# Turning k and q in halves in the first layer's PSUM banks, and using idle score banks at the end

## The chip, the cores and the metric

The kernel runs on one core of a Trainium2 chip. The metric is device time in microseconds, the median of three runs: 531.08 us for the kernel before (531.07 to 531.32). Its profiled execution has a span of 530.9 us, with TensorE's clock granted in full all the way.

## What is computed

Two stages. First attention over 8 batches of 8 heads, 576 positions of 64 numbers each, in which every score that lies more than `tau` below its row's greatest is dropped; then a two-layer network on the 4608 tokens, 512 to 2048 to 512, with `h - tanh(h)` between.

```python
def _attn_ref(q, k, v, tau):
    scale = 1.0 / np.sqrt(q.shape[-1])
    scores = scale * np.matmul(q, k.transpose(0, 1, 3, 2))
    thresh = np.max(scores, axis=-1, keepdims=True) - tau
    scores = np.where(scores >= thresh, scores, -1000000000.0)
    scores = scores - np.max(scores, axis=-1, keepdims=True)
    attn = np.exp(scores)
    attn = attn / (np.sum(attn, axis=-1, keepdims=True) + 1e-09)
    return np.matmul(attn, v).astype(np.float32)

def _moe_ref(x, w_in, w_out):
    h = x @ w_in
    g = h - np.tanh(h)
    return (g @ w_out).astype(np.float32)
```

## The kernel before

The heads are taken in 32 pairs, each of 9 score tiles of 128 queries (288 tiles in all). The main loop has one **slot** for each tile. In slot s TensorE makes the scores of tile s + 8, a step of the two-layer network (below), the value products of an earlier tile, and, in some slots, the turns of k or q of a coming pair. VectorE scales the scores and takes their maxima (`sc`), ScalarE makes from them the cut scores `z` and the weights `pT` and the `tanh` of the network's hidden layer, and GpSimd splits q and k into two fp16 parts and copies k's turned matrix with its halves swapped (`kS`). From pair 6 on the weights are turned by DMA (`zT`), and from pair 8 on three q of four too.

The network is done in 8 blocks of 512 tokens and a ninth with the 64 rows that are left of each batch. An **h step** (`hidden`) is four matmuls of the first layer into a bank of `ps_h`; its tanh (`bend`) and the subtraction that gives `g` (`shrink`) are issued in the next slot, and only `shrink` lets the bank go. A **y step** (`project`) is four matmuls of the second layer into the one bank of `ps_y`; four y steps make one output tile. A block's steps lie beside the scores of later pairs; the last two blocks come after all the scores.

[...]`ps_big` has two tiles of two banks, for scores and here for turns; `ps_o` one bank for value products; `ps_h` two for the first layer, and for turning x (`psX`); `ps_y` one for the second layer. A tile with the same tag waits for the one that had its place.

```python
    ps_big = pool("ps_big", 2, space=PSUM)
    ps_o = pool("ps_o", 1, space=PSUM)
    ps_h = pool("ps_h", 2, space=PSUM)
    ps_y = pool("ps_y", 1, space=PSUM)
    # ... (cut)
    def turn(p, t):
        hl = hls.pop((p, t))
        if t == "q" and q_by_dma(p):
            m = mats[p, t] = qk_pool.tile([P, W], FP16, name=f"{t}T", tag=t)
            nc.sync.dma_start_transpose(
                out=m.rearrange("p (c r) -> p c r", c=TPP),
                in_=hl.rearrange("p c a d -> p (c a d)"),
            )
            return
        ps = ps_big.tile([P, W], FP16, name=f"ps_{t}", tag="big")
        for c in range(TPP):
            turn_chunk(
                ps[:, c * P : (c + 1) * P], c, hl[:, c, :, :].rearrange("p a d -> p (a d)")
            )
        m = qk_pool.tile([P, W], FP16, name=f"{t}T", tag=t)
        nc.vector.tensor_copy(out=m, in_=ps)
        mats[p, t] = m
        if t == "k":
            sw = qk_pool.tile([P, W], FP16, name="kS", tag="ks")
            for lo, hi in ((0, D), (D, 0)):
                o, i = sw[lo : lo + D, :], m[hi : hi + D, :]
                nc.gpsimd.tensor_copy(out=o, in_=i)
            mats[p, "ks"] = sw
    # ... (cut)
    # scores(i), cut
        ps = ps_big.tile([P, 1024], F32, name="psS", tag="big")
    # ... (cut)
        sc = sc_pool.tile([P, S], F32, name="sc")
        nc.vector.tensor_scalar(
            out=sc, in0=ps[:, lo : lo + S], scalar1=SC, scalar2=None,
            op0=ALU.mult, op1=ALU.max, accum_out=mx[:, c : c + 1],
        )
    # ... (cut)
    # attend(i), cut
        if t == 1:
            ops[p, hh] = ps_o.tile([P, 6, D + 1], F32, name="psO", tag="o")
            if p % 2 and hh == 0:
                attend_shared(p, 1, pts.pop(i - 2))
        po = ops[p, hh]
    # ... (cut)
    def hidden(m, n, ps):
        if n == 0:
            gs[m] = g_pool.tile([P, DF_C, MB], BF16, name="g")
        for c in range(DM_C):
            nc.tensor.matmul(
                out=ps, lhsT=w_in_sb[:, c, n * P : (n + 1) * P],
                rhs=xs[m][:, c, :] if m < B else xR[:, c, :, :],
                start=(c == 0), stop=(c == DM_C - 1),
            )
        halves.append((m, n, ps))

    halves, ths = [], []

    def bend():
        while halves:
            m, n, ps = halves.pop(0)
            th = t_pool.tile([P, MB], F32, name="th")
            nc.scalar.activation(out=th, in_=ps, func=ACT.Tanh)
            ths.append((m, n, ps, th))

    def shrink():
        while ths:
            m, n, ps, th = ths.pop(0)
            nc.vector.scalar_tensor_tensor(
                out=gs[m][:, n, :], in0=th, scalar=-1.0, in1=ps,
                op0=ALU.mult, op1=ALU.add,
            )
    # ... (cut)
    # layers(m, tail), cut
        def h_step(n):
            if tail and n % 2:
                ps = ps_big.tile([P, MB], F32, name="psHt", tag="big")
            else:
                ps = ps_h.tile([P, MB], F32, name="psH", tag="h")
            hidden(m, n, ps)

        def y_step(m, ms, part):
            if part == 0:

                odd = tail and (m, ms) > (B - 2, 1) and ms % 2 == 0
                pl, tag = (ps_o, "o") if odd else (ps_y, "y")
                ys[m, ms] = pl.tile([P, d_model], F32, name="psY", tag=tag), odd
            ps, odd = ys[m, ms]
            project(m, ms, part, ps, odd)
    # ... (cut)
    # the loop over slots, cut
    turns = set()
    for p in range(HPAIR + 1, NPAIR):
        d = 6 if p % 2 else 3
        turns.add(TPP * p - AHEAD - (d if p >= 5 else 5))

    # ... (cut)
            assert not todo
            todo = layers(stage, False)
            room = range(s, min(s + HPAIR * TPP, NTILE))
            if room[-1] + 1 < NTILE:
                room = [a for a in room if a not in turns]
            share = len(todo) / len(room)
            done, stage = 0.0, stage + 1
    # ... (cut)
        n = s + AHEAD
        if 0 < n < NTILE and place(n)[1] is None and kind(n) == "B":
            scores(n - 1)
        if 0 <= n < NTILE and (place(n)[1] is not None or kind(n) == "B"):
            scores(n)
    # ... (cut)
        for i in kinks.pop(s, []):
            kink(i)
        bend()
        for i in wts.pop(s, []):
            weights(i)
        if 0 <= s < NTILE + FIRST:
            if todo and (s >= NTILE or s in room):
                done += share
                if s < NTILE and s == room[-1]:
                    done = 1e9
                while todo and done >= 1:
                    todo.pop(0)()
                    done -= 1
        if s == 0:
        shrink()
    # ... (cut)
            pp, jj = divmod(i, TPP)
            if i < NTILE:
                attend(i)
                odd = pp % 2
                if jj == 3 + odd:
                    norm(pp, 0)
                elif odd and jj in (0, 8):
                    norm(pp - (jj == 0), 1)
            if pp and jj == 1 + pp % 2:
                emit_x(pp - 1)
        for step in plan.pop(s, []):
            step()
        if s + AHEAD in cast_when:
            w_cast()
        if s + AHEAD in load_when:
            w_load(next(pieces))
```

Of the kernel before, what the change touches and what calls it, by code (L numbers as in the profile page):

```python
# [9 lines left out]
F32 = mybir.dt.float32  # L10
BF16 = mybir.dt.bfloat16
FP16 = mybir.dt.float16
# [6 lines left out]
def kernel(  # L19
# [216 lines left out]
    def turn_chunk(out, c, lhsT):  # L236
# [4 lines left out]
            out=out, lhsT=lhsT, rhs=rhs, is_transpose=True, start=True, stop=True  # L241
        )

    def q_by_dma(p):

        return p >= 2 * HPAIR and p % 4 != 0
# [7 lines that stand above are left out]
                in_=hl.rearrange("p c a d -> p (c a d)"),  # L254
            )
            return
        ps = ps_big.tile([P, W], FP16, name=f"ps_{t}", tag="big")
        for c in range(TPP):
            turn_chunk(
                ps[:, c * P : (c + 1) * P], c, hl[:, c, :, :].rearrange("p a d -> p (a d)")  # L260
            )
        m = qk_pool.tile([P, W], FP16, name=f"{t}T", tag=t)
        nc.vector.tensor_copy(out=m, in_=ps)
        mats[p, t] = m
        if t == "k":
            sw = qk_pool.tile([P, W], FP16, name="kS", tag="ks")
# [4 lines that stand above are left out]
# [138 lines left out]
    def attend(i):  # L409

        if kind(i) == "A":
            return
        p, hh, t = place(i)
        vb, pt = vbs[p % NV], pts[i]
        if hh is None:

            attend_shared(p - 1, 0, pt)
            return
        if t == 1:
            ops[p, hh] = ps_o.tile([P, 6, D + 1], F32, name="psO", tag="o")  # L420
            if p % 2 and hh == 0:
                attend_shared(p, 1, pts.pop(i - 2))
        po = ops[p, hh]

        nc.tensor.matmul(  # L425
            out=po[:, t - 1 : t + 1, :], lhsT=pt[:, 4 * P : 5 * P],
            rhs=vb[:, hh, 4:6, :], start=True, stop=False, skip_group_check=True,
        )
        for n in range(8):
            ab, c = divmod(n, 4)  # L430
            blk = 5 * ab + c
            nc.tensor.matmul(  # L432
                out=po[:, t - 1 + ab, :], lhsT=pt[:, blk * P : (blk + 1) * P],
                rhs=vb[:, hh, c, :], start=False, stop=(n == 7), skip_group_check=True,
            )
        pts.pop(i)
# [113 lines left out]
                    )  # L550


    EARLY = lambda m: 3 if m else 3
    LAST = 1

    FIRST = 3
    quarters = lambda m: [(m, ms, part) for ms in range(4) for part in range(4)]

    def layers(m, tail):


        def h_step(n):
# [8 lines that stand above are left out]

                odd = tail and (m, ms) > (B - 2, 1) and ms % 2 == 0
                pl, tag = (ps_o, "o") if odd else (ps_y, "y")
                ys[m, ms] = pl.tile([P, d_model], F32, name="psY", tag=tag), odd
            ps, odd = ys[m, ms]
            project(m, ms, part, ps, odd)

        def y_half(h):

            n = d_model // 2  # L580
            pl, tag = ((ps_y, "y"), (ps_o, "o"))[h]
            ps = pl.tile([P, n], F32, name="psY", tag=tag)
            for part in range(4):
                project(m, 3, part, ps, h == 0, slice(h * n, h * n + n))

        now = quarters(m - 1)[EARLY(m - 1) :] if m > 0 else []
        if m < NMB - 1:
            now += quarters(m)[: EARLY(m)]
        else:
            now += quarters(m)[:12]  # L590
        n = 16 + len(now)


        ahead = n - max(0, EARLY(m) - 3) - LAST if m < NMB - 1 else n - 9 - LAST
        steps, at, i = [], [], 0

        def ready(y):
            last = 4 * y[2] + 3
            return y[0] < m or len(at) > (last if m else 15) and at[last] + 2 < i

        while now or len(at) < 16:
            if len(at) < 16 and (
                not now or not ready(now[0]) or len(at) * ahead <= i * 16
            ) and not (m == B - 1 and i < FIRST):
                steps.append(lambda a=len(at): h_step(a))
                at.append(i)
            elif ready(now[0]):
                steps.append(lambda y=now.pop(0): y_step(*y))
            else:
                steps.append(lambda: None)  # L610
            i += 1
        if m == NMB - 1:
            steps += [lambda h=h: y_half(h) for h in range(2)]
        return steps

    ys = {}


    def w_pieces():
# [39 lines left out]
    for p in range(1, NPAIR):  # L659
        first = TPP * p - AHEAD  # L660
        for d, f in PREP[3 if p == 1 else 0 :]:
            d -= p == 1 and d in (3, 5)
            if d in (7, 8) and q_by_dma(p):
                d = d + 2
            if p in (2, 4):
                d = {8: 9, 7: 8, 5: 6}.get(d, d)
            elif d == 5 and p >= 5:
                d = 6 if p % 2 else 3
            plan.setdefault(first - d, []).append(lambda p=p, f=f: f(p))
        d = 7 if q_by_dma(p) else 3 - (p == 1 or p >= 5)  # L670
        d = 4 if p in (2, 4) else d
        plan.setdefault(first - d, []).append(lambda p=p: turn(p, "q"))
# [21 lines left out]

    turns = set()
    for p in range(HPAIR + 1, NPAIR):
        d = 6 if p % 2 else 3
        turns.add(TPP * p - AHEAD - (d if p >= 5 else 5))  # L700

    kinks, wts, atts = {}, {}, {}
    for i in range(NTILE + 3):
# [5 lines left out]
    for s in range(-AHEAD, NTILE + LAG + 3):  # L709
        p, j = divmod(max(s, 0), TPP)  # L710
        if 0 <= s < NTILE and j == 2 + LAG and p % HPAIR == 0 and p >= HPAIR:
            assert not todo
            todo = layers(stage, False)
            room = range(s, min(s + HPAIR * TPP, NTILE))
            if room[-1] + 1 < NTILE:
                room = [a for a in room if a not in turns]
            share = len(todo) / len(room)
            done, stage = 0.0, stage + 1
        if s == NTILE:
            todo = layers(stage, True)  # L720
            share, done, stage = 1, 0.0, stage + 1
        if 0 <= s + AHEAD - 1 < NTILE:
            shift(s + AHEAD - 1)

# [5 lines that stand above are left out]
        if s == 1 - AHEAD:  # L730
            for t in ("k", "q", "ks"):
                turn_first(t, 1)
        for i in kinks.pop(s, []):
            kink(i)
        bend()
        for i in wts.pop(s, []):
            weights(i)
        if 0 <= s < NTILE + FIRST:
            if todo and (s >= NTILE or s in room):
                done += share  # L740
                if s < NTILE and s == room[-1]:
                    done = 1e9
                while todo and done >= 1:
                    todo.pop(0)()
                    done -= 1
        if s == 0:
            nc.vector.tensor_tensor(
                out=fold, in0=ident_bf[:, 0:64], in1=ident_bf[:, 64:P], op=ALU.add
            )
        shrink()  # L750
        for store in stores[:-1]:
            store()
        del stores[:-1]
        for i in atts.pop(s, []):
# [14 lines that stand above are left out]
        if s + AHEAD in load_when:  # L769
            w_load(next(pieces))  # L770

    for step in todo:
        step()
        bend()
        shrink()
# [49 lines left out]
```

## Time and profile before

| | PE | DVE | ACT | POOL |
|---|---|---|---|---|
| busy, us of 530.9 | 507.7 | 422.1 | 433.4 | 289.3 |
| share | 96% | 80% | 82% | 54% |

PE is TensorE, PEld its weight loads (which lie beside its matmuls), DVE VectorE, ACT ScalarE, POOL GpSimd. Lines such as L331 are lines of the kernel; a name pair `psS<-kT,qT` is what an instruction writes and what it reads, `x2` how many instructions one row of a timeline stands for. A bracket at a row's end gives the engine's idle time before it and whose work ended it. Matmuls are pipelined and their ends are modelled, so two neighbouring matmuls overlap in the profile; their starts are firm.

Some durations that the text uses:

| row | instruction | count | mean ns |
|---|---|---|---|
| L341 | DVE scales a tile of scores, `sc<-psS` | 288 | 753 |
| L517 | DVE `g<-th,psH` | 128 | 684 |
| L263 | DVE `kT<-ps_k`, 1152 columns | 31 | 751 |
| L537 | DVE `yo<-psY` | 30 | 691 |
| L458 | DVE `osb<-psO,rc` (norm; with its reciprocal, 177) | 64 | 424 |
| L511 | ACT `th<-psH` | 128 | 583 |
| L368 | ACT `z<-sc` | 288 | 769 |
| L404 | ACT `pT<-zT` | 117 | 1154 |

### The profile page before, as it was taken

The page shows a single profiled execution, that of the slowest core. Times are in us where ns is not written, and L with a number is a line of the kernel's source. Part 1 is how long each engine was busy: PE and PEld are TensorE (multiplying, and loading weights), DVE is VectorE, ACT ScalarE, POOL GpSimd, SP SyncE. Part 2 cuts the span into 40 slices and gives each one's busy share as a digit, 9 for nine tenths or more (in the row PEclk, how much of TensorE's full clock was granted, in tenths as well). Part 3 has the DMA queues.
Part 4 walks back from the last instruction along what each step waited for, and adds up shares of the span by engine and source line. Part 5 has one row for each costly group of instructions (what it writes and reads, how often), then busy time and mean ns, then how long its engine had stood idle before and what let it go on. Part 6 is the DMA issues. An engine that isn't in the chain of part 4 may idle for free.

```text
span 530.9 us, 12707 instructions
## 1 busy us (share of the span) xinstructions
PE 507.7 (96%) x4606; PEld 286.4 (54%) x4606; DVE 422.1 (80%) x1179; ACT 433.4 (82%) x617; POOL 289.3 (54%) x390
## 2 busy tenths in 40 slices
PE   8999899989999989999999999999999999999996
PEld 4666566554555545555555555555555555444444
DVE  5999889997898878998889888888899887554440
ACT  5999999998898989988998989899998989544330
POOL 7999999684738366574738383846657430000000
PEclk9999999999999999999999999999999999999999
DMA  7843668989799999899998999999988976400113
GB/s 215 242 141 112 216 214 168 184 145 201 180 199 162 183 181 202 167 193 205 180 198 180 199 175 216 157 198 185 204 169 196 202 133 110 105 36 25 39 41 80
DMA packets 208607, 86.79 MB, mean 163 GB/s; under 512 B 176160, under 2 KB 200992, under 8 KB 208544
## 3 DMA queue, kind: packets, MB, share of 16 engines
q1 hardware_dynamic: 207952, 85.56, 77.4%
q8 instruction: 36, 0.59, 0.5%
q10 hardware_dynamic: 592, 0.43, 0.3%
q14 instruction: 27, 0.22, 0.1%
HBM read 36.70 MB, written 9.44 MB: 87 GB/s over the span
## 4 chain that ended last, share of the span: by engine, by line
PE 48%; issue 13%; ACT 12%; DVE 12%; POOL 7%; DMA 7%; SPq 1%; ACTq 0%; POOLq 0%; DVEq 0%
PE psY L524 15%; PE psH L498 12%; PE psS L331 9%; ACT z L368 5%; DVE sc L341 4%; ACT pT L396 3%; DMA zT<-z 3%; PE psHt L498 3%; DVE g L517 2%; PE psO L432 2%; ACT th L511 2%; POOL kS L269 2%; ACT pT L404 2%; DMA vraw<-in_v_dram 2%; PE psS L322 2%
## 5 line engine op out<-in xcount | busy, mean ns | idle before, releaser
L341 DVE TENSOR_SCALAR_CACHE_REDUCE sc<-psS 128x576 f32<-128x576 f32 x288 | 212.9, 753 | 34.2 <-PE psS L331 21.3
L368 ACT ACTIVATE z<-sc,nb 128x576 bf16<-128x576 f32 x288 | 216.0, 769 | 27.6 <-DVE nb L353 27.1
L524 PE MATMUL psY<-w_out_sb,g 128*128 128x512 bf16 (+1 forms) x592 | 146.0, 374 | 0.8 <-DVE yo L537 0.8
L404 ACT ACTIVATE pT<-zT 128x1152 f16<-128x1152 bf16 x117 | 135.0, 1154 | 10.6 <-DMA zT<-z 10.4
L269 POOL COPY kS<-kT 64x1152 f16<-64x1152 f16 x62 | 70.8, 1142 | 125.4 <-DVE nb L353 123.7
L498 PE MATMUL psH<-xT,w_in_sb 128*128 128x512 bf16 x480 | 123.3, 379 | 0.7 <-DVE g L517 0.3
L331 PEld LDWEIGHTS <-qT 128*128 128x128 f16 x1024 | 75.1, 97 | 67.3 <-issue 11.8
L331 PE MATMUL psS<-kT,qT 128*128 128x512 f16 (+1 forms) x512 | 104.3, 285 | 7.2 <-DVE sc L341 4.0
L517 DVE SCALAR_TENSOR_TENSOR g<-th,psH 128x512 bf16<-128x512 f32 x128 | 87.6, 684 | 25.5 <-ACT th L511 23.6
L331 PE MATMUL psS<-kS,qT 128*128 128x512 f16 x496 | 101.3, 286 | 1.7 <-POOL kS L269 1.6
L511 ACT ACTIVATE th<-psH 128x512 f32<-128x512 f32 x128 | 74.6, 583 | 21.9 <-PE psH L498 21.8
L524 PEld LDWEIGHTS <-g 128*128 128x128 bf16 x592 | 51.0, 98 | 57.2 <-issue 3.5
L498 PEld LDWEIGHTS <-w_in_sb 128*128 128x128 bf16 x576 | 48.8, 98 | 53.2 <-issue 1.0
L432 PE MATMUL psO<-vb,pT 128*128 128x65 bf16 x1024 | 53.3, 194 | 0.0
L432 PEld LDWEIGHTS <-pT 128*128 128x128 f16 x1024 | 44.2, 98 | 9.4
L193 POOL TENSOR_TENSOR khl<-kraw,khl 128x576 f16<-128x576 f32 x31 | 39.7, 1281 | 2.6
L193 POOL TENSOR_TENSOR qhl<-qraw,qhl 128x576 f16<-128x576 f32 x31 | 39.7, 1280 | 2.6
L396 ACT ACTIVATE pT<-psZ 128x512 f16<-128x512 bf16 (+1 forms) x54 | 35.1, 654 | 2.6 <-PE psZ L387 2.1
L537 DVE COPY yo<-psY 128x512 f32<-128x512 f32 (+1 forms) x31 | 21.1, 682 | 13.6 <-PE psY L524 12.4
L458 DVE TENSOR_TENSOR osb<-psO,rc 128x256 bf16<-128x256 f32 x64 | 27.2, 424 | 2.2
L425 PE MATMUL psO<-vb,pT 128*128 128x130 bf16 x128 | 28.1, 220 | 0.6 <-DVE nb L353 0.6
L387 PE MATMUL psZ<-ident_bf,z 128*128 128x128 bf16 x243 | 22.5, 220 | 2.1 <-ACT pT L396 1.3
(79 smaller groups left out, 509.5 us busy)
## 6 DMA issues: line engine op xcount, KB each, us to landing
vraw<-in_v_dram SPq DMA_DIRECT2D x32, 256.0 KB, 3.6
out_dram<-yo SPq DMA_DIRECT2D x32, 256.0 KB, 3.1
kraw<-in_k_dram SPq DMA_DIRECT2D x31, 256.0 KB, 3.1
qraw<-in_q_dram SPq DMA_DIRECT2D x31, 256.0 KB, 3.4
wt<-in_moe_w_in_dram SPq DMA_DIRECT2D x8, 512.0 KB, 4.6
wt<-in_moe_w_out_dram SPq DMA_DIRECT2D x8, 512.0 KB, 4.2
zT<-z SPq DMA_TRANSPOSE x117, 3.7
qraw<-in_q_dram SPq DMA_DIRECT2D x32, 32.0 KB, 3.1
```

Source lines behind the costliest of these rows:

```text
L193: nc.gpsimd.tensor_tensor(out=hl[:, :, 1, :], in0=x, in1=hl[:, :, 0, :], op=ALU.subtract)
L269: nc.gpsimd.tensor_copy(out=o, in_=i)
L331: nc.tensor.matmul(out=ps[:, dst], lhsT=lhs, rhs=kk[:, src], start=(n == 0), stop=(n == 1),)
L341: nc.vector.tensor_scalar(out=sc, in0=ps[:, lo : lo + S], scalar1=SC, scalar2=None, op0=ALU.mult, op1=ALU.max, accum_out=mx[:, c : c + 1],)
L368: nc.scalar.activation(out=z, in_=sc, func=ACT.Prelu, bias=nb, scale=1.0, alpha=STEEP)
L396: nc.scalar.activation(out=pt[:, off * P : (off + n) * P], in_=ps[:, 0 : n * P], func=ACT.Exp)
L404: nc.scalar.activation(out=pt[:, 0 : n * P], in_=zts.pop(i)[:, 0:n, :], func=ACT.Exp)
L432: nc.tensor.matmul(out=po[:, t - 1 + ab, :], lhsT=pt[:, blk * P : (blk + 1) * P], rhs=vb[:, hh, c, :], start=False, stop=(n == 7), skip_gr ...
L498: nc.tensor.matmul(out=ps, lhsT=w_in_sb[:, c, n * P : (n + 1) * P], rhs=xs[m][:, c, :] if m < B else xR[:, c, :, :], start=(c == 0), stop= ...
L511: nc.scalar.activation(out=th, in_=ps, func=ACT.Tanh)
L517: nc.vector.scalar_tensor_tensor(out=gs[m][:, n, :], in0=th, scalar=-1.0, in1=ps, op0=ALU.mult, op1=ALU.add,)
L524: nc.tensor.matmul(out=ps, lhsT=gs[m][:, n, ms * P : (ms + 1) * P], rhs=w_out_sb[:, n, cols], start=(n == 0), stop=(n == DF_C - 1),)
```

## The change

From pair 6 on, k, and q where TensorE turns it, are no longer turned as nine chunks in one tile of the score banks with one copy out. They go as five chunks and four, in two tiles of the first layer's pool `ps_h`, each with its own copy. That leaves both score tiles to the scores. k's turn is moved: for even pairs it comes one slot earlier, for odd ones one slot later, so that it falls on a slot without value products.

The network's steps are no longer spread by a running share. A list of slots (without those in which k is turned) is given to `layers`, which puts an h step or a y step on each: h steps are spread so that they end five slots before the list does, a y step is preferred in the slot just before a turn, and what is left goes into the last slot. In the last score stage the slots of turns are now left out too, so 29 slots are there for 32 steps.

Two tiles move to the score banks at the end, where scores are over: the value products of the last pair, and the first output tile of block 6.

```diff
--- before.py
+++ after.py
@@ -241,6 +241,14 @@
             out=out, lhsT=lhsT, rhs=rhs, is_transpose=True, start=True, stop=True
         )
 
+
+    BYHALF = HPAIR + 2
+
+    def k_lead(p):
+        if p < BYHALF:
+            return 6 if p in (2, 4) or p == HPAIR + 1 else 5 - (p == 1)
+        return 5 if p % 2 else 4
+
     def q_by_dma(p):
 
         return p >= 2 * HPAIR and p % 4 != 0
@@ -254,13 +262,20 @@
                 in_=hl.rearrange("p c a d -> p (c a d)"),
             )
             return
-        ps = ps_big.tile([P, W], FP16, name=f"ps_{t}", tag="big")
-        for c in range(TPP):
-            turn_chunk(
-                ps[:, c * P : (c + 1) * P], c, hl[:, c, :, :].rearrange("p a d -> p (a d)")
-            )
         m = qk_pool.tile([P, W], FP16, name=f"{t}T", tag=t)
-        nc.vector.tensor_copy(out=m, in_=ps)
+        if p < BYHALF:
+            spans, pl, tag = ((0, TPP),), ps_big, "big"
+        else:
+            spans, pl, tag = ((0, 5), (5, TPP)), ps_h, "h"
+        for c0, c1 in spans:
+            n = (c1 - c0) * P
+            ps = pl.tile([P, n], FP16, name=f"ps_{t}", tag=tag)
+            for c in range(c0, c1):
+                turn_chunk(
+                    ps[:, (c - c0) * P : (c - c0 + 1) * P], c,
+                    hl[:, c, :, :].rearrange("p a d -> p (a d)"),
+                )
+            nc.vector.tensor_copy(out=m[:, c0 * P : c1 * P], in_=ps)
         mats[p, t] = m
         if t == "k":
             sw = qk_pool.tile([P, W], FP16, name="kS", tag="ks")
@@ -417,7 +432,9 @@
             attend_shared(p - 1, 0, pt)
             return
         if t == 1:
-            ops[p, hh] = ps_o.tile([P, 6, D + 1], F32, name="psO", tag="o")
+
+            pl, tag = (ps_big, "big") if p == NPAIR - 1 else (ps_o, "o")
+            ops[p, hh] = pl.tile([P, 6, D + 1], F32, name="psO", tag=tag)
             if p % 2 and hh == 0:
                 attend_shared(p, 1, pts.pop(i - 2))
         po = ops[p, hh]
@@ -550,13 +567,14 @@
                     )
 
 
-    EARLY = lambda m: 3 if m else 3
+    EARLY = lambda m: 3
     LAST = 1
 
     FIRST = 3
     quarters = lambda m: [(m, ms, part) for ms in range(4) for part in range(4)]
 
-    def layers(m, tail):
+
+    def layers(m, tail, slots=None):
 
 
         def h_step(n):
@@ -571,6 +589,8 @@
 
                 odd = tail and (m, ms) > (B - 2, 1) and ms % 2 == 0
                 pl, tag = (ps_o, "o") if odd else (ps_y, "y")
+                if (m, ms) == (B - 2, 0):
+                    pl, tag = ps_big, "big"
                 ys[m, ms] = pl.tile([P, d_model], F32, name="psY", tag=tag), odd
             ps, odd = ys[m, ms]
             project(m, ms, part, ps, odd)
@@ -597,6 +617,21 @@
         def ready(y):
             last = 4 * y[2] + 3
             return y[0] < m or len(at) > (last if m else 15) and at[last] + 2 < i
+
+        if slots is not None:
+            for nth, i in enumerate(slots):
+                spare = len(slots) - nth - (16 - len(at)) - len(now)
+                can = now and ready(now[0]) and (m or i >= CAST_BY[now[0][2]])
+                due = len(at) * (len(slots) - OWN(m)) <= nth * 16
+                lull = i + 1 not in slots and spare >= 0
+                if len(at) < 16 and not (can and (lull or not due)) and (due or spare <= 0):
+                    steps.append((i, lambda a=len(at): h_step(a)))
+                    at.append(i)
+                elif can:
+                    steps.append((i, lambda y=now.pop(0): y_step(*y)))
+            assert len(at) == 16 and all(ready(y) for y in now)
+            steps += [(i, lambda y=y: y_step(*y)) for y in now]
+            return steps
 
         while now or len(at) < 16:
             if len(at) < 16 and (
@@ -616,6 +651,10 @@
     ys = {}
 
 
+    CAST_BY = (56, 56, 58, 64)
+    OWN = lambda m: EARLY(m) + 2
+
+
     def w_pieces():
         for w, sb, n in ((moe_w_in, w_in_sb, DM_C), (moe_w_out, w_out_sb, DF_C)):
             flat = sb.rearrange("p c n -> p (c n)")
@@ -659,13 +698,13 @@
     for p in range(1, NPAIR):
         first = TPP * p - AHEAD
         for d, f in PREP[3 if p == 1 else 0 :]:
-            d -= p == 1 and d in (3, 5)
+            d -= p == 1 and d == 3
             if d in (7, 8) and q_by_dma(p):
                 d = d + 2
-            if p in (2, 4):
-                d = {8: 9, 7: 8, 5: 6}.get(d, d)
-            elif d == 5 and p >= 5:
-                d = 6 if p % 2 else 3
+            if d == 5:
+                d = k_lead(p)
+            elif p in (2, 4):
+                d = {8: 9, 7: 8}.get(d, d)
             plan.setdefault(first - d, []).append(lambda p=p, f=f: f(p))
         d = 7 if q_by_dma(p) else 3 - (p == 1 or p >= 5)
         d = 4 if p in (2, 4) else d
@@ -694,10 +733,7 @@
 
 
 
-    turns = set()
-    for p in range(HPAIR + 1, NPAIR):
-        d = 6 if p % 2 else 3
-        turns.add(TPP * p - AHEAD - (d if p >= 5 else 5))
+    turns = {TPP * p - AHEAD - k_lead(p) for p in range(HPAIR + 1, NPAIR)}
 
     kinks, wts, atts = {}, {}, {}
     for i in range(NTILE + 3):
@@ -710,15 +746,12 @@
         p, j = divmod(max(s, 0), TPP)
         if 0 <= s < NTILE and j == 2 + LAG and p % HPAIR == 0 and p >= HPAIR:
             assert not todo
-            todo = layers(stage, False)
             room = range(s, min(s + HPAIR * TPP, NTILE))
-            if room[-1] + 1 < NTILE:
-                room = [a for a in room if a not in turns]
-            share = len(todo) / len(room)
-            done, stage = 0.0, stage + 1
+            todo = layers(stage, False, [a for a in room if a not in turns])
+            stage += 1
         if s == NTILE:
-            todo = layers(stage, True)
-            share, done, stage = 1, 0.0, stage + 1
+            todo = [(s + n, step) for n, step in enumerate(layers(stage, True))]
+            stage += 1
         if 0 <= s + AHEAD - 1 < NTILE:
             shift(s + AHEAD - 1)
 
@@ -735,14 +768,8 @@
         bend()
         for i in wts.pop(s, []):
             weights(i)
-        if 0 <= s < NTILE + FIRST:
-            if todo and (s >= NTILE or s in room):
-                done += share
-                if s < NTILE and s == room[-1]:
-                    done = 1e9
-                while todo and done >= 1:
-                    todo.pop(0)()
-                    done -= 1
+        while todo and todo[0][0] <= s < NTILE + FIRST:
+            todo.pop(0)[1]()
         if s == 0:
             nc.vector.tensor_tensor(
                 out=fold, in0=ident_bf[:, 0:64], in1=ident_bf[:, 64:P], op=ALU.add
@@ -769,7 +796,7 @@
         if s + AHEAD in load_when:
             w_load(next(pieces))
 
-    for step in todo:
+    for _, step in todo:
         step()
         bend()
         shrink()
```

## The prediction

> **What bounds the kernel now.** I read the engine shares first, then windows cut at the shared score tiles (one every 18 tiles), then TensorE's waits in the steady part, then its timeline around the turns.
>
> ```profile
> PE 507.7 (96%) x4606; PEld 286.4 (54%) x4606; DVE 422.1 (80%) x1179; ACT 433.4 (82%) x617; POOL 289.3 (54%) x390
> ...
> 203.30:232.10 28.80, 28.54 (x266) 16.06 (x267) 25.63 (x73) 25.91 (x36) 17.25 (x23) 1.00 0.97 187
> ...
> 463.00:500.00 37.00, 37.00 (x173) 16.76 (x172) 17.57 (x28) 14.90 (x25) 0.00 (x0) 1.00 0.10 36
> ```
>
> The columns of a window are its length, then the busy time of PE, PEld, DVE, ACT and POOL, the clock and DMA. In the steady part PE is busy 28.54 of 28.80 us, ACT 25.91 and DVE 25.63; after 463 us PE is busy without a break. TensorE is the bound, at full clock, and what is not its own work is a stall of it. A matmul's shown end is modelled and hides gaps, so I take stalls from starts: next start minus this start minus what the group costs back to back.
>
> ```profile
> PE ps_k L240 <- DVE sc L341: 1.2, 7, 0.2
> PE psS L331 <- POOL kS L269: 1.0, 3, 0.3
> PE psS L331 <- DVE sc L341: 0.5, 1, 0.5
> ...
> 213.78 0.41 PE L432 MATMUL psO<-vb,pT 128*128 128x65 bf16 x8
> 214.37 0.66 PE L240 MATMUL ps_k<-ident_f,khl 128*128 128x128 f16 x9 [0.17 <-DVE sc L341]
> 215.05 0.41 PE L331 MATMUL psS<-kT,qT 128*128 128x512 f16 x2
> ...
> 253.04 0.67 PE L240 MATMUL ps_k<-ident_f,khl 128*128 128x128 f16 x9
> 254.18 0.41 PE L331 MATMUL psS<-kT,qT 128*128 128x512 f16 x2 [0.47 <-DVE sc L341]
> ```
>
> Eight value products cost 0.26 us (208.33 to 208.59) and nine turns 0.51 (224.53 to 225.04). So the turn at 214.37 came 0.33 late, waiting for one of the two score banks, and the scores behind it at 215.05 another 0.17; at 254.18 they came 0.63 late. From 203.3 to 261.2, four pairs of heads, the turns cost: 0.33 + 0.17, again 0.33 + 0.17 at 243.1, 0.63, the q turn at 216.4 0.04 + 0.23, and 0.49 at 247.6 for the swapped copy of k: 2.4 us in 57.9. That is all that this part of the change can win there, per four pairs.
>
> **What the Trainium skill says.** "Perfetto Trace Analysis", Optimization Strategy: the same gap repeated on the engine that should be saturated can mean that there isn't enough SBUF or PSUM for the next tile. The trace agrees: `ps_k <- DVE sc` is seven waits of nearly equal length. "PSUM — Partial Sum Buffer", Engine vs sequencer instructions: VectorE's queue is strictly first in, first out, and matmuls start and complete in program order. The trace agrees (kT's copy at 156.97 stands behind sc at 155.57 and g at 156.37), and my argument rests on it. "VectorE: DVE Perf Modes", Why PSUM operands drop a tier: a PSUM operand leaves at most the mode that packs two 16-bit elements. The trace agrees: 1152 fp16 are copied in 751 ns, 576 fp32 scaled in 753.
>
> **The change part by part.** I listed slot by slot (a slot is one score tile) what TensorE is given before and after.
>
> *k in halves.* From pair 6 on, the nine turns go into two tiles of the first layer's pool, which has two banks. TensorE's work is the same. DVE gets two copies in place of one:
>
> ```profile
> L263 DVE COPY kT<-ps_k 128x1152 f16<-128x1152 f16 x31 | 23.3, 751 | 1.1 <-PE ps_k L240 0.9
> L291 DVE COPY kT<-ps_k 128x640 f16<-128x640 f16 x1 | 0.5, 491 | 0.9 <-PE ps_k L240 0.9
> L488 DVE COPY xT<-psX 128x512 bf16<-128x512 bf16 x32 | 13.4, 420 | 1.8 <-PE psX L481 1.8
> ```
>
> 0.49 + 0.42 = 0.91 us against 0.75, for 26 k turns and 8 q turns: 34 x 0.16 = 5.4 us of DVE, beside other work (DVE has 3 of 28.8 us free). The waits on score banks go. The turn's slot gets no layer step, and even pairs turn a slot earlier, which also gives POOL's kS time: I count the whole 2.4 us as won.
>
> But both first-layer banks are now full when the next step of the first layer comes, and in nearly every case it comes in the very next slot. Take slot 78 (k of pair 10), starting at t. Scores of tile 86 t to 0.49 (two 0.24 groups), turns to 0.99, in slot 79 scores of tile 87 to 1.48, then h step 1 of block 1, which wants a bank. On DVE the first half's copy stands behind tile 86's scaling, and that can't begin before the scores are there:
>
> ```profile
> 167.73 0.41 PE L331 MATMUL psS<-kT,qT 128*128 128x512 f16 x2
> ...
> 168.51 0.76 DVE L341 TENSOR_SCALAR_CACHE_REDUCE sc<-psS 128x576 f32<-128x576 f32 x1 [0.34 <-PE psS L331]
> ```
>
> 0.78 here, 0.69 at 152.21 (scores from 151.52). With 0.70: scaling to 1.46, copy to 1.95, and 0.06 to signal (sc ended 155.65, ps_k began 155.71). The h step starts at 2.01, not 1.48: **0.53 us lost at each k turn**, even with DVE caught up. DVE often isn't. Walked with the rows' durations from the slot before: pair 10's kind has an output copy (0.69), a g (0.68) and a norm (0.60) in the slot before, so the second half waits 0.5 for its bank and the h step 1.2: 1.7. Pair 11's kind has psX in the other bank: 0.2 + 0.7 = 0.9. Pair 12's kind 1.05, pair 13's 0.7.
>
> *q in halves.* From pair 8 on only every fourth q is turned by TensorE, now in a slot that has an h step of its own, with another just before (slots 97 and 98 for pair 12). Its first half waits for the earlier h step's g: scores at t, h step 0.49 to 1.35; DVE scaling 0.70 to 1.46, g to 2.14. The first half starts at 2.15 instead of 1.35, 0.8 lost. The second half can't have the bank of the h step just given, whose tanh is only issued in the next slot, so it takes the first half's bank after its copy: turns end 2.43, result 0.17 later, copy to 3.1, start 3.15 instead of 2.43, 0.72 lost. Together **1.5 us**, for pairs 12, 16, 20, 24 and 28.
>
> *Sum for four pairs.* Least: 4 x 0.53 + 1.5 = 3.6 new against 2.4 gone, +1.2. Walked with DVE's backlog: 1.7 + 0.9 + 1.05 + 0.7 + 1.6 = 5.95, +3.55. The truth should lie between, as a TensorE that waits lets DVE catch up; I take the middle, +2.4. Pairs 10 to 31 are 5.5 such fours: +13.
>
> *Pairs 6 to 9.* Old stalls about 3.5 us by starts (1.37 the longest); new, 4 x 0.53 for k and three q turns of about 0.8, 4.5 at least, 7.8 if walked. TensorE also waits for pT there, 0.2 to 0.3 at a time, which hides some: +2.
>
> *The end.* The last pair's value products take idle score banks, and so does the first output tile of block 6.
>
> ```profile
> 453.54 0.45 PE L443 MATMUL psO<-vb,pT 128*128 128x130 bf16 x5 [0.28 <-DVE osb L463]
> ...
> 460.28 1.02 PE L524 MATMUL psY<-w_out_sb,g 128*128 128x512 bf16 x4 [0.78 <-DVE yo L537]
> ```
>
> By starts these lost 0.44 and 0.95; both waits should go: -1.4 us. The last score stage has 29 slots for its 32 layer steps, so three steps fall into its last slot. The order changes, the work doesn't: 0. After 463 us nothing changes.
>
> Sum: 531.1 + 13 + 2 - 1.4 = 544.7, say 545 us.
>
> **Rivals.** *Freed score banks win.* If the h step after a turn found a bank, because copies run sooner than I think, the 2.4 us per four pairs would be gained, 13 us by pair 31, with the end about 516. For it: the waits on sc are real, and the new plan puts a y step ahead of a turn where it can. Against: two banks, two halves, and the copy's place in DVE's order. *Nothing moves.* Stalls swap places and ACT (25.9 of 28.8) holds the pace: 529 to 533, the end's 1.4 us showing alone. Against it: ACT has 2.9 us free in each window, so a TensorE stall isn't covered. *DVE becomes the bound.* 5.4 us more of copies, 0.3 per 18 tiles: DVE goes to about 26 of 28.8, so no, save in 88 to 117 us, where it is busy 27.25 of 29.
>
> **Range and chances.** The least sum gives 531 + 6.6 + 0 - 1.4 = 536, the walked one 531 + 19.5 + 4.3 - 1.4 = 553. I widen to 533 and 556 for durations and overlaps that I don't know. 2% above is 541.7, inside the range and below its middle: slower 0.62, same 0.35. Faster needs 10.6 us of the 13 that could at most be won with no new wait: 0.03.
>
> **What would show it.** Right: TensorE's waits gain `psH <- DVE kT` (and qT) of 0.4 to 1 us, some 20 times, and `ps_q <- DVE g` and `ps_q <- DVE qT`; `ps_k <- DVE sc` is gone; the steady window grows from 28.9 to 29.5 to 30.7 us for 18 tiles; the waits at 453 and 460 are gone. Wrong: windows of 28 us, or h steps that start straight after the scores in the slot behind a turn. The weakest steps are how far DVE is behind at a turn, and that the half's copy really comes after that slot's scaling.

## The result and the profile after

The changed kernel takes 550.6 us (median of 4 runs, 549.94 to 551.79) against 531.2 (531.07 to 531.45): ratio 1.0367, 95% interval 1.0348 to 1.0386. It is slower by 19.4 us; the two profiled executions differ by 17.3 (spans of 548.2 and 530.9), as the profiled one of the kernel before took 532.69 us, 1.5 over the median, and that of the changed kernel 549.94, 0.7 under its own median.

The engines' busy times of the changed kernel, from its page, then two windows (length; busy time of PE, PEld, DVE, ACT, POOL; clock; DMA share; GB/s), one in the steady part and one after the last scores:

```profile
PE 510.5 (93%) x4606; PEld 287.3 (52%) x4606; DVE 424.4 (77%) x1213; ACT 436.1 (80%) x617; POOL 290.2 (53%) x390
...
209.80:240.40 30.60, 28.59 (x264) 16.00 (x263) 26.24 (x76) 26.37 (x37) 17.09 (x23) 1.00 0.86 171
...
480.30:517.30 37.00, 37.00 (x175) 16.75 (x173) 17.48 (x27) 14.87 (x25) 0.00 (x0) 1.00 0.10 37
```

No engine has much more work; VectorE, with 34 more copies, is busy 424.4 us against 422.1. The window of 18 tiles that took 28.8 us takes 30.6 here, with the same 28.6 us of TensorE in it; the part after the scores is as it was. So TensorE waits more, and only beside the scores. What it waits for, from its waits (total us, times, longest):

```profile
PE psH L515 <- DVE kT L278: 10.4, 22, 0.8
PE ps_k L240 <- DVE g L534: 5.6, 10, 1.6
PE ps_q L240 <- DVE g L534: 4.5, 6, 1.0
PE ps_q L240 <- DVE qT L278: 4.1, 7, 0.6
```

`ps_k <- DVE sc`, of which the prediction shows seven even waits, is gone. In its place stand four waits on the first layer's two banks. TensorE's timeline shows them for pair 16, whose q TensorE turns as it does for pair 12 (start, modelled length, and in brackets the visible idle time; matmuls' starts are what to reckon with):

```profile
218.84 0.67 PE L240 MATMUL ps_k<-ident_f,khl 128*128 128x128 f16 x9
219.34 0.41 PE L346 MATMUL psS<-kT,qT 128*128 128x512 f16 x2
219.59 0.41 PE L346 MATMUL psS<-kS,qT 128*128 128x512 f16 x2
220.49 1.02 PE L515 MATMUL psH<-xT,w_in_sb 128*128 128x512 bf16 x4 [0.49 <-DVE kT L278]
...
222.15 1.03 PE L515 MATMUL psH<-xT,w_in_sb 128*128 128x512 bf16 x4
223.86 0.44 PE L240 MATMUL ps_q<-ident_f,qhl 128*128 128x128 f16 x5 [0.69 <-DVE g L534]
224.88 0.38 PE L240 MATMUL ps_q<-ident_f,qhl 128*128 128x128 f16 x4 [0.58 <-DVE qT L278]
```

The turns now start at once and so do the scores behind them (219.34). But the h step that could start at 219.83 starts at 220.49: 0.66 us. The h step at 222.15 ends its issue at 223.01, and q's first half follows at 223.86 (0.85); five turns take 0.28, and its second half comes at 224.88 instead of 224.14 (0.74).

For the next-but-one pair, 18, both engines are shown, in order of time:

```profile
248.90 0.69 DVE L554 COPY yo<-psY 128x512 f32<-128x512 f32 x1
...
249.50 0.45 PE L240 MATMUL ps_k<-ident_f,khl 128*128 128x128 f16 x5
249.51 0.68 DVE L534 SCALAR_TENSOR_TENSOR g<-th,psH 128x512 bf16<-128x512 f32 x1
...
250.24 0.38 PE L240 MATMUL ps_k<-ident_f,khl 128*128 128x128 f16 x4 [0.29 <-DVE g L534]
250.31 0.42 DVE L475 TENSOR_TENSOR osb<-psO,rc 128x256 bf16<-128x256 f32 x1
...
250.72 0.75 DVE L356 TENSOR_SCALAR_CACHE_REDUCE sc<-psS 128x576 f32<-128x576 f32 x1
...
251.39 0.81 DVE L278 COPY kT<-ps_k 128x640 f16<-128x640 f16 x2
...
251.93 1.02 PE L515 MATMUL psH<-xT,w_in_sb 128*128 128x512 bf16 x4 [0.82 <-DVE kT L278]
```

The first half's turns were all issued by 249.78. Its copy comes at 251.39, since VectorE has an output copy, a g, a norm and that slot's scaling in front of it, and the h step waits for it.

Where the time goes, by the starts of the shared score tiles:

| stretch, from tile to tile | before, us | after, us | more, us |
|---|---|---|---|
| 44 to 98 | 84.6 (60.01 to 144.60) | 89.1 (60.25 to 149.33) | 4.5 |
| 98 to 134 | 58.7 | 60.4 | 1.8 |
| 134 to 170 | 57.9 | 60.6 | 2.7 |
| 170 to 206 | 57.4 | 60.1 | 2.7 |
| 206 to 242 | 57.3 | 60.1 | 2.8 |
| 242 to 278 | 58.4 | 61.1 | 2.7 |
| 278 to the end | 96.6 | 96.5 | -0.1 |

The first two rows understate the loss. The profile before has a wait in each that another profile of the same code doesn't have (the run with the end alone, below, is the same up to tile 278):

```profile
137.62 0.41 PE L331 MATMUL psS<-kT,qT 128*128 128x512 f16 x2 [1.15 <-DVE sc L341]
...
196.29 0.41 PE L331 MATMUL psS<-kT,qT 128*128 128x512 f16 x2 [1.25 <-DVE sc L341]
```

Some 4 us before each of them ScalarE had waited (2.08 and 2.19 us) for weights that DMA turned; its tanh, then VectorE's g and scaling, then these scores came after that. Against that other profile the two stretches grew by 5.8 and 3.1 us.

### The profile page after: what moved, and what is told of

It is laid out like the page before. It is cut to its first block, busy times and chain, and to the rows that moved or that the text cites. A ratio compares the mean times of both kernels' runs of the same rounds, so it can differ in the third digit from the quotient of the medians.

```text
span 548.2 us, 12680 instructions
## 1 busy us (share of the span) xinstructions
PE 510.5 (93%) x4606; PEld 287.3 (52%) x4606; DVE 424.4 (77%) x1213; ACT 436.1 (80%) x617; POOL 290.2 (53%) x390
## 4 chain that ended last, share of the span: by engine, by line
PE 67%; DVE 13%; ACT 9%; issue 6%; POOL 3%; DMA 2%; SPq 0%; ACTq 0%; DVEq 0%; POOLq 0%
PE psY L541 20%; PE psH L515 18%; PE psS L346 13%; DVE sc L356 4%; PE psO L449 4%; DVE g L534 3%; ACT z L383 3%; PE psHt L515 3%; ACT pT L411 2%; PE psS L337 2%; ACT pT L419 2%; DMA zT<-z 2%; DVE kT L278 1%; PE ps_q L240 1%; ACT th L528 1%
## 5 line engine op out<-in xcount | busy, mean ns | idle before, releaser
L383 ACT ACTIVATE z<-sc,nb 128x576 bf16<-128x576 f32 x288 | 219.7, 770 | 42.3 <-DVE nb L368 40.0
L515 PE MATMUL psH<-xT,w_in_sb 128*128 128x512 bf16 x480 | 123.6, 380 | 11.7 <-DVE kT L278 10.4
L346 PEld LDWEIGHTS <-qT 128*128 128x128 f16 x1024 | 72.5, 98 | 51.6 <-issue 3.5
L515 PEld LDWEIGHTS <-w_in_sb 128*128 128x128 bf16 x576 | 50.7, 98 | 68.0 <-issue 15.1
L240 PE MATMUL ps_k<-ident_f,khl 128*128 128x128 f16 x288 | 24.0, 220 | 6.7 <-DVE g L534 5.6
```

Source lines behind the costliest of these rows:

```text
L346: nc.tensor.matmul(out=ps[:, dst], lhsT=lhs, rhs=kk[:, src], start=(n == 0), stop=(n == 1),)
L383: nc.scalar.activation(out=z, in_=sc, func=ACT.Prelu, bias=nb, scale=1.0, alpha=STEEP)
L515: nc.tensor.matmul(out=ps, lhsT=w_in_sb[:, c, n * P : (n + 1) * P], rhs=xs[m][:, c, :] if m < B else xR[:, c, :, :], start=(c == 0), stop= ...
```

## The experiments

Two theories. **Queue**: what costs the time is that a bank which TensorE wants back is released only when VectorE's queue comes to its copy, behind the scaling of the same slot and whatever is left from the slot before, while TensorE has too little to do meanwhile. **Bank**: the first layer's two banks are simply too few. Others: the new order of layer steps, VectorE's extra copies, the new place of the turns. Each run is compared with the kernel before on the same chip.

**Copies alone.** Two copies instead of one, nothing moved.

```diff
-        nc.vector.tensor_copy(out=m, in_=ps)
+        if p >= HPAIR + 2:
+            for c0, c1 in ((0, 5), (5, TPP)):
+                nc.vector.tensor_copy(out=m[:, c0 * P : c1 * P], in_=ps[:, c0 * P : c1 * P])
+        else:
+            nc.vector.tensor_copy(out=m, in_=ps)
```

> The kernel before, but from pair 6 on each whole turn of k and q is copied out of its score bank in two copies, 640 and 512 columns, as the halves are. Nothing else moves. Theory: the copies' extra VectorE time is beside other work, within 1 us of the kernel before. Rival (VectorE's load is what the halves cost): 3 us or more above it.

531.44 us, ratio 1.0001 (0.9989 to 1.0014). VectorE's extra copying, 5 us by the copies' durations and 1.8 by its busy time (423.9 against 422.1), costs nothing here; its load alone is out as a cause.

**Halves at the old slots.** Kernel before, with the halves in `ps_h` as in the change.

```diff
-        ps = ps_big.tile([P, W], FP16, name=f"ps_{t}", tag="big")
         # ... (cut)
-        nc.vector.tensor_copy(out=m, in_=ps)
+        if p < HPAIR + 2:
+            spans, pl, tag = ((0, TPP),), ps_big, "big"
+        else:
+            spans, pl, tag = ((0, 5), (5, TPP)), ps_h, "h"
+        # ... (cut: the loop over spans, as in the change)
```

> The kernel before, with only the halves: from pair 6 on k, and q where TensorE turns it, in two tiles of the first layer's banks, at the old slots and with the old order of layer steps. Theory: a first-layer step or psX lies in the slot before or in the slot of each k turn, so the halves wait for its g or its copies, about 1 us per k turn, and q loses little as a second-layer step is in its slot: 543 to 550 us. Rival, the old slots had work beside the turn and so hide the halves' waits: 529 to 535 us.

545.94 us, 1.0268 (1.0246 to 1.0289). In the range of the theory, against its rival. TensorE's waits of this run:

```profile
PE ps_k L240 <- DVE g L524: 17.1, 15, 1.5
PE ps_k L240 <- DVE xR L496: 5.9, 11, 0.7
```

Here the halves wait for the h step or psX that sits in the slot before or in their own; `psH <- kT` doesn't show among its waits: the halves have already waited, and behind most of these turns lies a y step. At these slots the choice of the bank alone costs 14 us. That doesn't part the two theories: VectorE's queue sets when a bank comes free, but a third bank might have made the wait harmless, and no run gave the first layer one.

**Slots alone.** Kernel before, whole turns in the score banks, only k's slots moved.

```diff
+    KL = lambda p: 6 if p == 5 else 5 if p % 2 else 4
     # ... (cut)
-                d = 6 if p % 2 else 3
+                d = KL(p)
     # ... (cut: the same in the list of turns)
```

> The kernel before, whole turns in the score banks and its running share of layer steps, with only k's turns moved to the changed kernel's slots. Theory: the moved slot has only scores and a turn, so the next scores meet a bank whose scaling is not done, 0.5 us or more per turn, as in the run with whole turns at the new slots: 538 to 543 us. Rival, that run's 10 us came from the new order of layer steps: 530 to 533 us.

542.93 us, 1.0209 (1.0187 to 1.0231), in the range of the theory. So the new slots alone cost 11 us, without any halves:

```profile
PE psS L331 <- DVE sc L341: 23.6, 30, 2.0
```

A slot with nothing but scores and a turn sends TensorE to the next scores before the scaling is done. Moving k away from the value products took its cover away.

**Whole turns in the changed kernel.**

```diff
-        if p < BYHALF:
+        if True:
             spans, pl, tag = ((0, TPP),), ps_big, "big"
```

> The changed kernel, but with k and q turned whole in the score banks in every pair, at the changed kernel's slots and with its order of layer steps. Theory (a turn's bank comes back only after its slot's scaling and copy, and the changed slot gives TensorE nothing to do meanwhile): the waits of psH for kT go, but with only scores and a turn in the slot the next scores meet the same copies' order one bank further, psS waiting for sc by at least 0.5 us at each k turn; the q turns lose only about 0.2 us each, so some 7 us come back: 541 to 545 us. Rival, the choice of bank alone is the cause: all of it comes back and the time is about 530 us. Second rival, the new order of layer steps by itself costs the time: it stays at 548 to 551 us.

541.13 us, 1.0173 (1.0147 to 1.0199), in the range of the queue theory and against both rivals. The wait has only changed its name:

```profile
PE psS L346 <- DVE sc L356: 19.3, 32, 1.4
```

Beside the run before it (542.93; old order of steps, old end, and like this one without a layer step in the turn's slot) the new order of layer steps costs nothing in sum. It isn't neutral everywhere: by starts, tiles 98 to 278 take 294.4 us here against 298.2 there, tiles 44 to 98 88.5 against 85.3, of which 2.2 is a single wait for weights (`psO <- pT`).

**Only q whole.**

```diff
-        if p < BYHALF:
+        if p < BYHALF or t == "q":
```

> The changed kernel, but q alone is turned whole in the score banks; k stays in halves. Theory: each of the five q turns from pair 12 on gains about 1.3 us (1.6 lost by halves against 0.25), those of pairs 6 to 8 about 0.5: 542 to 544 us, and no psH or ps_q wait for qT. Rival, the k turns carry all of the loss and q's waits only move: 549 to 551 us.

540.44 us, 1.0158 (1.0129 to 1.0187), better than the 542 to 544 expected. The two `ps_q` waits that had stood for 8.6 us are gone, and `psH <- kT` is as it was:

```profile
PE psH L515 <- DVE kT L278: 10.4, 22, 0.8
```

The halves of eight q turns cost some 10 us. And since k whole (541.1) and k in halves (540.4) are alike at these slots, the halves of k cost next to nothing of their own there: the slot did.

**k ahead of its slot's scores.** The changed kernel, with k's turns and copies issued before the scores, so that the copies pass the scaling in VectorE's queue.

```diff
+            ahead_ = f is PREP[5][1] and p >= BYHALF
+            (early if ahead_ else plan).setdefault(first - d, []).append(lambda p=p, f=f: f(p))
     # ... (cut)
+        for step in early.pop(s, []):
+            step()
         n = s + AHEAD
```

> The changed kernel, but from pair 6 on k's nine turns and their two copies are issued ahead of the scores of their slot, so that the copies stand ahead of that slot's scaling in VectorE's queue. Theory: the waits of psH for kT (10.4 us in all) go nearly all; the second half asks for its bank half a microsecond earlier and waits longer for the g before it (ps_k for g, 5.6 us, grows); net about 1 us per four pairs back: 543 to 547 us. Rival, the place in VectorE's queue does not matter and the copies are simply too slow: the waits for kT stay above 8 us and the time at 549 to 551.

547.75 us, 1.0317 (1.0286 to 1.0349). `psH <- kT` is gone altogether, which shows that the place behind the slot's scaling made that wait. What stands now:

```profile
PE ps_k L240 <- DVE g L534: 8.2, 12, 0.9
...
PE ps_k L240 <- DVE nb L368: 2.8, 6, 0.8
```

Most of it moved to the turns, which ask for their bank half a microsecond sooner: some 3 us were won, just under the 3.6 to 7.6 expected. So that place explains the named wait, but not by itself the 19 us.

**A y step in each turn's slot.** Halves as in the change; a fixed list puts a y step ahead of each turn and no h step in the slot before.

```diff
-            todo = layers(stage, False, [a for a in room if a not in turns])
+            todo = layers(stage, False, list(room))
+   # 36 slots of a block, turns in 2, 10, 20, 28 (k) and 22 (q):
+   "y-yhhyhyh-yhhyhyhyh-yhyhhyh-yhhyhyyy"
```

> The changed kernel with its halves in the first layer's banks and its turns' slots kept, but the layer steps are put on slots by a fixed list: a second-layer step goes into each slot of a k or q turn ahead of it, no first-layer step into the slot before a k turn, and the free slots lie before turns. Theory: the copy is covered by that step (0.86 us against 0.53), psH waits for kT go and the q turn keeps about 0.5 us: some 20 us come back, 524 to 530 us. Rival, two banks are too few for halves, first-layer tiles and psX in whatever order: 540 us or more.

540.27 us, 1.0155 (1.0129 to 1.0182): a miss, by 10 us, and in the range of the rival that two banks are too few in whatever order. Where the covering y step was not the last of an output tile, the h step mostly came at most 0.2 us late; where VectorE had an output copy or a norm ahead of k's copies, 0.6 to 1.3. VectorE's rows around one of those (a `...` stands for rows left out), and the h step that waits:

```profile
215.67 0.75 DVE L356 TENSOR_SCALAR_CACHE_REDUCE sc<-psS 128x576 f32<-128x576 f32 x1
...
216.34 0.68 DVE L554 COPY yo<-psY 128x512 f32<-128x512 f32 x1
216.94 0.81 DVE L278 COPY kT<-ps_k 128x640 f16<-128x640 f16 x2
...
217.48 1.02 PE L515 MATMUL psH<-xT,w_in_sb 128*128 128x512 bf16 x4 [1.09 <-DVE kT L278]
```

My cover step had put its own output copy ahead of k's.

**Mended.** No last y step in a k turn's slot, q whole.

```diff
-   "y-yhhyhyh-yhhyhyhyh-yhyhhyh-yhhyhyyy"
+   "y-yhhhyhh-yhhyhyhyh-yhhyhyh-yhyhyyyy"
-        if p < BYHALF:
+        if p < BYHALF or t == "q":
```

> The run with covering steps, but no second-layer step that ends an output tile (and so puts its copy into VectorE's queue ahead of k's copies) shares a slot with a turn, and q is turned whole in the score banks. Theory (what stands in VectorE's queue ahead of k's copies sets when the bank comes back): the waits of psH for kT of 0.85 to 1.09 us shrink to about 0.1 and the q turn's 0.5 goes: 2.5 us per four pairs, some 13 us: 525 to 529 us, so faster than both kernels. Rival, the two banks stay too few: 536 us or more.

535.69 us, 1.0072 (1.0048 to 1.0096): better by 4.6 us, where I expected 11 to 15, so it beats the changed kernel but not the one before. `psH <- kT` fell from 11.4 to 3.8 us as it should, but a new wait took over, psX behind two h steps in a row:

```profile
PE psX L492 <- DVE g L534: 7.3, 7, 1.4
PE psH L515 <- DVE kT L278: 3.8, 7, 0.8
```

**Whole turns with cover.** Score banks for all turns, a layer step in each turn's slot, no two h steps just before psX.

```diff
+   "yhyhyhh-h-yhhyhyhyh-yhyhyhy-yhhyhyyy"
-        if p < BYHALF:
+        if True:
```

> The changed kernel's k slots, but k and q turned whole in the score banks, and a layer step ahead of the turn in each turn's slot, by a fixed list; no two first-layer steps just before psX. The tiles at the end as in the changed kernel. Theory (what is lost at a turn is the time in which TensorE has nothing to do while VectorE scales and copies, wherever the turn's bank lies; a layer step of 0.86 us covers it): the waits of psS for sc at the turns go, 2.4 us per four pairs under the kernel before, and 1.4 us at the end: 516 to 524 us, faster than both kernels. Rival (ScalarE and VectorE, at 90% in the steady part, take over as soon as TensorE waits less): 528 us or more.

530.79 us, 0.9995 (0.998 to 1.001): level with the kernel before, against my theory's 516 to 524 and in the rival's range. The 10 us that whole turns lost at these slots are won back, so what cost them was the slot without cover. What k's halves would cost with cover isn't shown: the mended run has them, at 535.7 us, but by another list. Of the wait, 19.3 us with whole turns alone, 9.0 stay, half a microsecond and more at turns that follow a slot without a step:

```profile
PE psS L346 <- DVE sc L356: 9.0, 17, 1.1
```

**Fed.** The free slots put behind the turns instead, so that TensorE doesn't run ahead of VectorE before them.

```diff
-   "yhyhyhh-h-yhhyhyhyh-yhyhyhy-yhhyhyyy"
+   "yhy-hyhyhyh-hyhhyhhyh-yhyhyyh-hyhyyy"
```

> As the run with whole turns and a layer step in each turn's slot, but that run left the slot before a turn without a step, so that TensorE ran ahead and VectorE (scaling, g and norm, 2 us) was behind when the turn's scaling came; here the slots without a step lie after the turns and each slot before a turn has one. Theory (how far VectorE is behind at the turn sets what is left): the seven waits of psS for sc of 0.4 to 0.9 us in the steady part go, 1.7 us per four pairs: 521 to 527 us. Rival (VectorE and ScalarE hold the pace, so stalls only move): 529 to 532 us.

533.56 us, 1.0031 (1.0018 to 1.0045), slightly slower. The named wait did go, from 9.0 to 1.9 us; others came:

```profile
PE psH L515 <- DVE g L534: 4.2, 8, 1.0
PE psS L346 <- DVE sc L356: 1.9, 5, 0.6
```

and, by starts, 0.28 us at scores behind a free slot (18 times), too short to show in the waits. My theory that a turn's own stall can be removed for good by order fell here: the stall moved to the next place where TensorE asks for a bank, as the rival has it, though the time lies above the rival's range too.

**The end alone.** Kernel before, the two tiles at the end in the score banks.

```diff
+            pl, tag = (ps_big, "big") if p == NPAIR - 1 else (ps_o, "o")
     # ... (cut)
+                if (m, ms) == (B - 2, 0):
+                    pl, tag = ps_big, "big"
```

> The kernel before, with only the two tiles at the end moved: the last pair's value products and the first output tile of block 6 in the score banks. Theory: the waits of 0.44 and 0.95 us near 453 and 460 us go and nothing takes their place: 1.4 us less, about 529.7 us. Rival, another wait at the same place (the norm of the last pair) takes over: 531 us.

530.56 us, 0.9987 (0.9975 to 0.9999): 0.6 us less where 1.4 was expected, and only just outside the noise. Both waits of 0.44 and 0.95 us are gone, and one of 0.44 by starts is new:

```profile
452.13 1.02 PE L499 MATMUL psH<-xT,w_in_sb 128*128 128x512 bf16 x4 [0.27 <-DVE g L518]
```

From the last shared score tile to the first `psHt` it takes 28.30 us against 29.25. It is the only version tried whose interval lies below both kernels, by a tenth of a per cent.

**By stage.** The spans of these runs' profiles, cut at the starts of the shared score tiles (us):

| run | tiles 44 to 98 | 98 to 278 | 278 to the end |
|---|---|---|---|
| kernel before | 84.6 | 289.7 | 96.6 |
| the end alone | 83.3 | 288.4 | 95.7 |
| changed kernel | 89.1 | 302.3 | 96.5 |
| halves at the old slots | 86.2 | 301.1 | 96.7 |
| slots alone | 85.3 | 298.2 | 96.6 |
| whole turns | 88.5 | 294.4 | 96.6 |
| only q whole | 88.4 | 294.0 | 96.6 |
| whole turns with cover | 85.1 | 286.4 | 97.3 |

From tile 98 to 278, q whole brings back 8.3 us, 1.7 for each of the five q turns there, and turning k whole as well brings no more. From 44 to 98 neither brings back much, so what is lost there isn't the halves alone. Whole turns with cover are 2 to 3 us faster than the kernel before from 98 to 278, and give back 0.5 to 1.8 in the stretch before and 0.7 to 1.6 at the end.

## Why the prediction was right

The range (533 to 556) held the result in its upper part, and slower by more than 2% was the likeliest of the three. The forecast was 13.6 us slower; the profiles show 17.3. Of the difference, 1.3 lies in tiles 44 to 98, 0.6 from 98 to 278 (12.6 against 12.0), 1.3 at the end and 0.2 before tile 44: the errors all point one way, so the sum wasn't saved by luck.

*The waits that go.* Right: `ps_k <- sc` is gone, and all of the 2.4 us could be counted as won, as the sum below shows.

*The wait that comes, and its place.* Right: 22 waits of psH for kT, 6 of ps_q for g, 7 for qT. The run with k ahead of the scores shows that the copy's place behind the slot's scaling is what holds the bank, which I had named a weak step.

*Sizes, per four pairs*, by starts from 209.8 to 270.4 us (pairs 16 to 19; least and walked are those of pairs 12, 13, 10 and 11, the same places in the cycle of four):

| | least | walked | measured |
|---|---|---|---|
| pair 16, k | 0.53 | 1.05 | 0.66 |
| pair 16, q | 1.5 | 1.6 | 0.85 + 0.74 = 1.59 |
| pair 17, k | 0.53 | 0.7 | 0.07 + 0.42 = 0.49 |
| pair 18, k | 0.53 | 1.7 | 0.46 + 0.99 = 1.45 |
| pair 19, k | 0.53 | 0.9 | 0.39 + 0.20 + 0.42 = 1.01 |
| sum | 3.6 | 5.95 | 5.20 |

5.20 less the 2.4 of before is 2.8, and the stretch grew by 2.7; I had taken 2.4. The term that was too small is how far VectorE is behind, which I put at the middle and which lay at two thirds of the way.

*Pairs 6 to 9.* Too small. From tile 44 to 98 the kernel lost 4.5 us, 5.8 against the other profile; I had 2 for these pairs and about 1.2 for pairs 10 and 11. The named waits are there, up to 1.6 us for a second half of k that waits for g, but as whole turns lose nearly as much in that stretch, the cause isn't settled. TensorE's clock was 0.94 from 91 to 121 us of the profile; the run with k ahead took 90.1 us for the stretch at a clock of 1.00, so it is long without that too.

*The end.* Right on the two waits, wrong in the sum: -0.1 us where I had -1.4. The stretch from tile 278 is as long as before, yet it holds two more layer steps (22 against 20 up to the last psX, as the slots of the last turns are left free), 1.7 us of TensorE. So the waits there gave back about 1.7 us; I had 1.4, but 0 for the order of steps, and that term was wrong by those 1.7. (The last score stage has 30 slots for its 32 steps, not 29; three steps do fall into the last one.) In the kernel before, the last stage didn't leave its turns' slots free, so turns 30 and 31 had cover there; that too went.

*What I did not see.* I put the whole loss down to the banks, and the empty slot only served to count the old waits as won. The runs divide it otherwise: the new slots alone cost 11 us with whole turns, the halves alone 14 at the old slots, and both together with the new order and the new end 19. k in halves and k whole are alike at the new slots, where a layer step in the turn's slot wins back the 10 us; q's halves make the other 10, from tile 98 to 278 at 1.7 a turn, where the starts show 1.59, of which a whole turn would keep some 0.25; the rest of the 1.7 is not traced. Whether q's halves cost that for their place in VectorE's queue or for want of a third bank was not tested.

## What to carry to other kernels

In these runs a buffer came free when the slower engine's queue reached the instruction that releases it (`psH <- kT`: 10.4 us with the copy behind the scaling, none with it ahead). So before a producer is moved to other banks, write down what stands ahead of its copy, and what the producing engine can do until then: a slot that looks idle, and so inviting, is where nothing covers the wait. Sum the stalls of the place you leave and of the place you go to with the same care: here, with TensorE, VectorE and ScalarE busy 28.5, 25.6 and 25.9 of 28.8 us, a stall taken away at one bank came back at the next in three of the runs (k ahead, mended, fed).

## What the runs showed that I had not expected

Turns whole in the score banks with a step in their slot halve their named wait (19.3 to 9.0 us) and still leave the time where it was (530.8 us), and shifting the free slots moved it up (533.6): from 530.8 to 535.7 us the order of steps matters most, and no list tried went clearly under the running share of the kernel before in the whole time. Whether VectorE's pace or that of the chain through ScalarE holds it there was not settled.
